# Gated linear attention and four experts in one kernel: hidden values moved by 128 bytes, K's right halves copied by GpSimd for six units, last stores in halves

## The chip, the cores and the metric

The kernel runs on one core of a Trainium2 chip. The metric is the time of one execution on the device in microseconds. Times of the kernel before are six runs: their median is 1057.78 us, the lowest 1056.80 and the highest 1058.26. A core has five engines with their own queues of instructions: TensorE (PE in the profile; PEld is its load of weights), VectorE (DVE), ScalarE (ACT), GpSimd (POOL) and SyncE (SP), which here does nothing but start transfers.

## What is computed

The first half is a gated linear attention: for each batch and head a state of 48 x 48 is scaled, row by row, with a gate, and a product of key and value is added; the output is the query times the state.

```python
# q, k, v, alpha: (4, 8, 768, 48), float32; alpha in 0.8 .. 1.0
for t in range(S):
    state = alpha[:, :, t, :, None] * state + einsum('bhd,bhe->bhde', k[:, :, t], v[:, :, t])
    y[:, :, t] = einsum('bhd,bhde->bhe', q[:, :, t], state)
```

The second half takes this output as 3072 rows `x` of 384 (8 heads of 48 side by side) and sends every row through four experts, whose results are added with normalised weights:

```python
# w1: (4, 384, 1024), w2: (4, 1024, 384)
p = domain_probs / (domain_probs.sum(-1, keepdims=True) + 1e-9)
for e in range(E):
    h = np.maximum(x @ w1[e], 0.0)
    out += p[:, e:e + 1] * (h @ w2[e])
```

## The kernel before

**Units and groups.** The sequence of 768 is cut into 6 chunks of 128 positions (`cb`); with 4 batches (`b`) this gives 24 *units* of 128 rows. `order` lists them chunk by chunk. The first group (`groups[0]`) holds 2 units, the next five hold 4 each, and the last (`LAST`, number 6) holds 2. A *task* is one expert on one group: `up` multiplies the group's `x` with `w1` and applies ReLU, `down` multiplies the hidden values with `w2`, and `add_up` adds the scaled result to the accumulator `acc`. The tasks of groups 0 to 4 follow one another; those of the last two groups alternate.

**Attention of a unit.** `attention(u)` is a generator. It transposes the gates, K and Q of all 8 heads on TensorE (`turned`, L270) into tiles `AT`, `KT` and `QT`, and then goes through seven levels of halving (`LEVELS`): on level `li`, blocks of `m` positions are joined in pairs. On each level `copy_q` (L321, ScalarE, two copies) copies the right halves of Q into a block tile `qb`, `next_q` (L328 and L330, VectorE) multiplies the right halves of Q and the gates with the gates of the left halves, and `next_k` (L341, VectorE) multiplies the left halves of K with the gates of the right halves. `next_k` writes a new `KT` tile, since TensorE still reads the old one, and so the right halves, which don't change, are copied over (L340). That is six copies of 128 x 256 elements for each unit. `products` (L348) multiplies K and Q of a level on TensorE, `take` (L358, VectorE) picks from the result by a mask, and `far` (L403) is the product of the highest level. `lat` holds the finished coefficients (L416, L421); `result` multiplies them with V and Q with the state (L443, `yps`), and L478 makes the product for the next state. The rows `x` go to `x_raw`.

**Order.** Engines work their queues in the order in which the program is written, and that order is written out by hand. For unit 0 and most of unit 1 it is a list of steps with idle products (`fill`) between them; TensorE has no other work then. From unit 1 on, the steps of an attention lie between the products of an expert task: `deal` gives each step a time from a table of costs, and `advance`, called with each product, inserts the steps that are due. So the attention of units 2 to 5, which are group 1, lies beside the experts of group 0, and so on. The weights are loaded once by SyncE (`load_piece`, L214 to L217), split by ScalarE and VectorE into three parts (`split_piece`, L226 to L232), and written by GpSimd's queue to device memory (L233, `kept<-w`); later groups load the split parts (L196, `w<-kept`). Raw pieces of `w2` lie in `hT` tiles of hidden values that aren't in use.

**In the experts.** L549 and L557 are the products with `w1` (`one`, `two`); L568, L570, L595 and L597 turn their sums into the hidden values `hT` in three parts (L551 for group 0, in one part), and L603 finishes the third. L650 is the product with `w2`, which takes 128 x 128 values of `hT` as the weights of TensorE and lets `w2` move through; L677 and L679 add up.

**Where tiles lie.** The pool `work` holds the tiles of the attention, `xT` and `x_raw`; the pool `hid` behind it holds `hT` and `acc`. In `work`, `x_raw` is the tile that is allocated last.

**Stores.** `add_up` puts the store of a finished unit on a list. The list is emptied in `up` of the next tasks, and what is left at the end of the program. GpSimd's queue starts the stores of groups 0 to 4, SyncE those of the last two.

Of the kernel before, what the change touches and what calls it, by code (L numbers as in the profile page):

```python
# [10 lines left out]
F32 = mybir.dt.float32  # L11
# [9 lines left out]
def kernel(  # L21
# [37 lines left out]
    nc = tc.nc  # L59

    B, H, S, D = q.shape
    E, DM, F = moe_w1.shape
    P = 128
# [5 lines left out]
    KC = DM // P  # L69
    FCH = F // P  # L70
    NT = B * P
# [6 lines left out]
    assert DM % P == 0 and F % (P * NQ) == 0 and DM <= 512 and KC * QF == FPQ * DM  # L78
    FINE = 1 + 1 / 4096
    TRIM = 1 - 1 / 8192  # L80

    j = np.arange(P)[:, None] % HALF
    n = np.arange(QUAD)[None, :]
# [7 lines left out]
    work = ctx.enter_context(tc.tile_pool(name="work", bufs=2))  # L91
# [20 lines left out]
    half = B // 2  # L112
    groups = [order[:half]] + [order[i:i + B] for i in range(half, len(order), B)]
    LAST = len(groups) - 1
# [20 lines left out]
    xraws = {}  # L135
# [4 lines left out]
    stores = deque()  # L140
# [80 lines left out]
    def split_piece(l, i):  # L221
# [3 lines left out]

        nc.scalar.activation(out=top, in_=whole, func=ACT.Copy, scale=TRIM)  # L226
        yield
        nc.scalar.activation(out=dif, in_=whole, func=ACT.Copy, scale=TRIM * 4096)
        yield
# [34 lines left out]
    def halves(t, m):  # L264
        return t.rearrange("p a (b two r) -> p a b two r", two=2, r=m)
# [7 lines left out]
    def attention(u):  # L273
# [15 lines left out]
        def own_terms():  # L289
            own = work.tile([P, NT], F32, name="t")[:, :H * D].rearrange("p (h d) -> p h d", d=D)  # L290
            nc.vector.tensor_mul(own, rq[:, :, :D], rk[:, :, :D])
            nc.vector.reduce_sum(out=dot, in_=own, axis=AX.X)
            load(after, "k")


        alone = u == 0
        if not alone:
            own_terms()
        yield
# [33 lines left out]
        def next_k(li):  # L333
            m = LEVELS[li]
            old = new = halves(KTs[li], m)
            if li + 1 < len(LEVELS):
                KTs.append(keys())
                new = halves(KTs[-1], m)
                copy = nc.gpsimd.tensor_copy if alone else nc.scalar.copy
                copy(out=new[:, :, :, 1, :], in_=old[:, :, :, 1, :])  # L340
            nc.vector.tensor_mul(new[:, :, :, 0, :], old[:, :, :, 0, :],  # L341
                                 spread(halved(decs[li])[:, :, :, 1], m))
# [24 lines left out]
        for li in range(3):  # L367
            copy_q(li)
            next_q(li)
            next_k(li)  # L370
            yield
# [6 lines left out]
        for li in range(4):  # L378
            products(li, banks[li // 2][:, li % 2])
        next_q(3)  # L380
        next_k(3)
        take(0, banks[0][:, 0])
        take(1, banks[0][:, 1])
        yield
        copy_q(4)
        next_q(4)
        next_k(4)
        take(2, banks[1][:, 0])
        take(3, banks[1][:, 1])
# [24 lines left out]
        for s in range(2):  # L414
            rows = slice(HALF * s, HALF * (s + 1))
            nc.scalar.copy(out=parts[:HALF, :, s, :, HALF:], in_=far[rows])  # L416
        yield
        for s in range(2):
            rows = slice(HALF * s, HALF * (s + 1))
            copy = nc.vector.tensor_copy if alone and s else nc.scalar.copy  # L420
# [8 lines left out]
        def result():  # L429
            yps = ps.tile([P, KC, P], F32, name="yps", tag="w")  # L430
            for c in range(KC):


                if c < 2:
                    now = [[(2 * c + j // 2, j % 2, (0, HD + TAIL)[j % 2], 2 * QUAD * (j % 2))
                            for j in range(4)]]
                    turns = ([(True, now[0])] if cb > 0 else []) + [(False, now[0])]
                else:
                    turns = [(True, [(p, 0, 0, QUAD) for p in range(NP)])] if cb > 0 else []
                    turns += [(False, [(p, i, QUAD + TAIL * i, 0) for p in range(NP)]) for i in range(2)]  # L440
                for n, (past, turn) in enumerate(turns):
                    for j, (p, i, in_v, in_st) in enumerate(turn):
                        nc.tensor.matmul(  # L443
                            yps[QUAD * j:QUAD * (j + 1), c, :],
                            lhsT=flat_st[:, p, in_st:in_st + QUAD] if past
                            else flat_v[:, p, in_v:in_v + QUAD],
                            rhs=QT[:, p, :] if past else lat[:, 2 * p + i, :],
                            start=(n == 0), stop=(n == len(turns) - 1))
            gi, slot = place[cb, b]
            if slot == 0:  # L450
                if gi == 0:
                    xTs[gi] = work.tile([P, 3, KC, NT], F32R, name="xT", bufs=1)
                    xraws[gi] = xTs[gi][:, 2].bitcast(F32)
                elif gi < LAST:
                    xraws[gi] = work.tile([P, KC, NT], F32, name="x_raw", bufs=1)
                else:
                    xraws[gi] = []
            if gi < LAST:
                nc.scalar.copy(out=xraws[gi][:, :, slot * P:(slot + 1) * P], in_=yps)
            else:  # L460

                xraws[gi].append(AT)
                nc.scalar.copy(out=AT[:, :KC, :], in_=yps)
# [6 lines left out]
        for step in (turn_keys, result) if u >= half else (result, turn_keys):  # L470
            step()
            yield

        if cb < NCB - 1:
# [5 lines left out]
            for i in range(2):  # L480
                rows = slice(HD * i, HD * (i + 1))
# [17 lines left out]
    def split_x(gi, step):  # L499
# [7 lines left out]
        for kc in range(KC) if step == 0 else [step - 1]:  # L507
# [3 lines left out]
            for x, out in pieces:  # L511
                if step == 0:
                    nc.scalar.activation(out=out[0], in_=x, func=ACT.Copy, scale=TRIM)
                else:
# [78 lines left out]
    def hidden_parts(x, parts):  # L593
        top, low, dif = parts
        nc.scalar.activation(out=top, in_=x, func=ACT.Relu, scale=TRIM)  # L595
        yield
# [13 lines left out]
    def down(gi, e, slots, between):  # L610
# [20 lines left out]
        for n, (side, slot, part, fc) in enumerate(steps):  # L631
            c, f = divmod(fc, FPQ)
            advance(cost(1, gi, e) * len(slots) / len(steps))
            while between and n >= between[0][0] * len(steps):
                between.popleft()[1]()
            if n and n % (len(steps) // (2 * len(slots))) == 0:
                background()
            if later and n % (len(steps) // 12 - 1) == len(steps) // 12 - 2:
                make_dif(*later.popleft())
            at = (side, slot)  # L640
            if n == begins[at]:
                sums[at] = ps.tile([P, DM], F32, name="ops", tag="g", bufs=4)
            h = hidden[c][:, :, f, slot * P:(slot + 1) * P]
            if part < 3:
                w = wt[1][first + c].rearrange("p t (c d) -> p t c d", d=DM)[:, part, f]
                h = h[:, part]
            else:
                w = wt[1][first + c].rearrange("p (c d) -> p c d", d=DM)[:, f]
                h = h[:, 2].bitcast(F32)
            nc.tensor.matmul(sums[at], lhsT=h, rhs=w, start=(n == begins[at]), stop=(n == ends[at]))  # L650
            if n == ends[at]:
                add_up(gi, e, slot, side, sums.pop(at))
# [14 lines left out]
    def add_up(gi, e, slot, kind, part):  # L667

        cb, b = groups[gi][slot]
        at = b * NCB + cb  # L670
        if e == 0 and (kind == 0 or not split2(gi, e)):
            accs[cb, b] = hid.tile([P, DM], F32, name="acc", bufs=B) if gi < LAST else \
                work.tile([P, NP * P], F32, name="QT")[:, :DM]
        acc = accs[cb, b]
        scale = (p_fine if kind == 0 else p_all)[:, at, e:e + 1]
        if e == 0 and (kind == 0 or not split2(gi, e)):
            nc.scalar.activation(out=acc, in_=part, func=ACT.Copy, scale=scale)  # L677
        else:
            nc.vector.scalar_tensor_tensor(out=acc, in0=part, scalar=scale, in1=acc,  # L679
                                           op0=ALU.mult, op1=ALU.add)  # L680
        if kind == 0:
            return
        if e == E - 1:
            del accs[cb, b]
            row = b * S + cb * P
            stores.append(lambda: (nc.sync if gi >= LAST - 1 else nc.gpsimd).dma_start(
                out=out[row:row + P, :], in_=acc))

# [43 lines left out]
    with tc.manual_schedule():  # L734
# [23 lines left out]
        def fill(n):  # L758
            for _ in range(n):
                nc.tensor.matmul(idle, lhsT=zeros, rhs=zeros, start=True, stop=True)  # L760

        runs = [attention(u) for u in range(len(groups[0]))]
        fill(7)
        for u, n in ((0, 2), (0, 3), (0, 4), (0, 5), (0, 5), (0, 4), (0, 3), (1, 0), (0, 0), (0, 2),
# [66 lines left out]
```

## Time and profile before

| | |
|---|---|
| Median of six runs | 1057.78 us (1056.80 to 1058.26) |
| The profiled execution | 1057.32 us, span 1055.5 us |
| Busy: TensorE, its weight loads | 1037.6 us, 903.2 us |
| Busy: VectorE, ScalarE, GpSimd | 781.8 us, 565.5 us, 35.5 us |
| Granted clock of TensorE | 1.000 |
| Transfers | 251.66 MB, mean 238 GB/s |

The profile is of one execution. The span reaches from its first to its last instruction; the execution is 1.82 us longer. In the lists, a line names its place in the kernel, the engine, the operation, what is written and read, and the shapes; behind the bar stand the busy time, the mean of one instruction in ns, and the idle time of the engine ahead of them with what ended it. In a timeline the first number is the start from the beginning of the span and the second the duration, both in us, and a bracket gives the idle time just before and what ended it. "SPq" is SyncE's queue.

How the busy time lies over the start (us in each stretch; the attention of units 0 and 1 fills the first two, that of units 2 to 5 lies in the next five):

| Stretch | PE | DVE | ACT | POOL | share of the transfer engines |
|---|---|---|---|---|---|
| 20 to 40 | 17.00 | 12.48 | 12.03 | 0.00 | 0.65 |
| 40 to 60 | 18.97 | 11.73 | 14.61 | 1.74 | 0.68 |
| 60 to 80 | 17.62 | 14.41 | 16.77 | 1.06 | 0.95 |
| 80 to 100 | 18.79 | 17.96 | 16.94 | 1.06 | 0.61 |
| 100 to 120 | 18.56 | 16.13 | 15.33 | 1.06 | 0.90 |
| 120 to 140 | 19.50 | 14.94 | 13.42 | 1.07 | 0.67 |
| 140 to 160 | 19.24 | 16.33 | 14.33 | 2.12 | 1.09 |

### The profile page before, as it was taken

To read this page: it belongs to the slowest core of one execution; us is meant where nothing else is said; L and a number is where in the kernel's file an instruction comes from. 1 tells how busy PE (TensorE), PEld (TensorE's weight loads), DVE (VectorE), ACT (ScalarE), POOL (GpSimd) and SP (SyncE) were. 2 spreads that over 40 slices of the span, in tenths; PEclk is the share of its full clock that TensorE was granted. 3 is DMA by queue.
4 is the path that set the end of the run, shared out by engine and by line. 5 is a ranking of instruction groups with operands and counts; after the bars stand their busy time and mean duration, and the time that the engine had idled before them with its cause. 6 is when DMAs were issued, how large, how long until landed. Compare 5 with 4: busy or idle time off the path is not lost.

```text
span 1055.5 us, 21578 instructions
## 1 busy us (share of the span) xinstructions
PE 1037.6 (98%) x8498; PEld 903.2 (86%) x8498; DVE 781.8 (74%) x1620; ACT 565.5 (54%) x1195; POOL 35.5 (3%) x77
## 2 busy tenths in 40 slices
PE   8899999999999999999999999999999999999998
PEld 8777777687877899898898898998989889898998
DVE  5578777668879778778877777986877875656565
ACT  4687876585665654445546536555474443323232
POOL 3000010000001000000000000000000000000000
PEclk9999999999999999999999999999999999999999
DMA  7696799997878956857759659586594454444531
GB/s 117 173 325 215 238 322 348 323 335 242 276 266 293 376 192 226 319 170 279 287 175 343 229 169 348 182 286 239 170 372 179 187 210 172 186 181 179 198 162 46
DMA packets 158838, 251.66 MB, mean 238 GB/s; under 512 B 120113, under 2 KB 135345, under 8 KB 136209
## 3 DMA queue, kind: packets, MB, share of 16 engines
q1 hardware_dynamic: 152688, 208.87, 58.0%
q0 software_dynamic: 5760, 41.29, 9.8%
q8 instruction: 67, 1.10, 0.4%
q14 instruction: 35, 0.28, 0.1%
q10 hardware_dynamic: 288, 0.12, 0.1%
HBM read 207.79 MB, written 42.47 MB: 237 GB/s over the span
## 4 chain that ended last, share of the span: by engine, by line
PE 85%; DVE 4%; ACT 4%; DMA 3%; SPq 2%; issue 1%; POOL 0%; ACTq 0%; DVEq 0%; POOLq 0%
PE ops L650 36%; PE one L557 23%; PE two L557 11%; PE sc L348 6%; PE yps L443 3%; PE tp L270 3%; DMA hT<-in_moe_w_dram 2%; ACT qb L321 1%; PE one L549 1%; PE sps L478 1%; PE far L403 1%; SPq L214 1%; DMA w<-in_moe_w_dram 1%; DVE w L230 1%; DVE near L358 1%
## 5 line engine op out<-in xcount | busy, mean ns | idle before, releaser
L650 PE MATMUL ops<-w,hT 128*128 128x384 f32 x1872 | 346.6, 340 | 0.2 <-DVE hT L603 0.2
L650 PEld LDWEIGHTS ops<-w,hT 128*128 128x128 f32 x1872 | 324.5, 188 | 4.7 <-ACT t L568 0.7
L557 PE MATMUL one<-xT,w 128*128 128x512 f32 x960 | 252.6, 398 | 0.9 <-DVE xT L252 0.5
L557 PEld LDWEIGHTS one<-xT,w 128*128 128x128 f32 x960 | 175.7, 188 | 39.2 <-ACT t L568 1.5
L568 ACT ACTIVATE t<-one 128x512 f32<-128x512 f32 (+1 forms) x192 | 107.0, 558 | 174.9 <-PE one L557 169.8
L321 ACT COPY qb<-QT 64x256 f32<-64x256 f32 x336 | 136.6, 406 | 73.7 <-DVE QT L300 40.9
L597 DVE SCALAR_TENSOR_TENSOR hT<-t,hT 128x512 fp32r<-128x512 f32 (+1 forms) x172 | 110.6, 643 | 68.2 <-ACT hT L595 65.7
L570 DVE TENSOR_TENSOR t<-t,two 128x512 f32<-128x512 f32 (+1 forms) x172 | 109.5, 637 | 57.7 <-ACT t L568 29.1
L595 ACT ACTIVATE hT<-t 128x512 fp32r<-128x512 f32 (+1 forms) x172 | 101.8, 592 | 85.7 <-DVE t L570 84.6
L557 PE MATMUL two<-xT,w 128*128 128x512 f32 x480 | 136.2, 392 | 0.0
L557 PEld LDWEIGHTS two<-xT,w 128*128 128x128 f32 x480 | 90.1, 188 | 20.0 <-DVE acc L679 0.3
L650 PE MATMUL ops<-hT 128*128 128x384 f32 x288 | 100.9, 491 | 0.3 <-DMA hT<-in_moe_w_dram 0.3
L603 DVE SCALAR_TENSOR_TENSOR hT<-hT 128x512 fp32r<-128x512 f32 (+1 forms) x172 | 101.0, 635 | 0.0
L358 DVE COPY_PREDICATED near<-masks,sc 128x256 f32<-128x256 uint8 x144 | 76.9, 534 | 19.2 <-PE sc L348 16.3
L328 DVE TENSOR_TENSOR QT<-QT,dec 128x256 f32<-128x256 f32 x144 | 61.2, 425 | 35.5 <-ACT qb L321 34.8
L348 PEld LDWEIGHTS sc<-qb,KT 128*64 128x64 f32 x2304 | 72.7, 138 | 9.3 <-issue 4.7
L348 PE MATMUL sc<-qb,KT 128*64 128x64 f32 x2304 | 77.2, 223 | 2.6 <-ACT qb L321 2.6
L650 PEld LDWEIGHTS ops<-hT 128*128 128x128 f32 x288 | 52.1, 190 | 29.6 <-DMA hT<-in_moe_w_dram 0.9
L679 DVE SCALAR_TENSOR_TENSOR acc<-ops,p_all,acc 128x384 f32<-128x384 f32 x82 | 49.9, 615 | 29.3 <-PE ops L650 28.2
L341 DVE TENSOR_TENSOR KT<-KT,dec 128x256 f32<-128x256 f32 x144 | 60.3, 419 | 0.0
L340 ACT COPY KT<-KT 128x256 f32<-128x256 f32 x138 | 57.5, 416 | 3.0
L549 PE MATMUL one<-xT,w 128*128 128x256 f32 (+1 forms) x240 | 46.9, 341 | 1.8 <-DMA w<-in_moe_w_dram 1.1
(90 smaller groups left out, 934.1 us busy)
## 6 DMA issues: line engine op xcount, KB each, us to landing
w<-kept SPq DMA_DIRECT2D x144, 1152.0 KB
kept<-w POOLq DMA_DIRECT2D x32, 1152.0 KB, 7.7
hT<-in_moe_w_dram SPq DMA_DIRECT2D x32, 384.0 KB
w<-in_moe_w_dram SPq DMA_DIRECT2D x48, 128.0 KB
ra<-in_alpha_dram SPq DMA_DIRECT2D x23, 192.0 KB
rk<-in_k_dram SPq DMA_DIRECT2D x23, 192.0 KB
rq<-in_q_dram SPq DMA_DIRECT2D x23, 192.0 KB
out_dram<-acc POOLq DMA_DIRECT2D x18, 192.0 KB, 7.0
```

Of the source, the lines that this page charges most:

```text
L321: nc.scalar.copy(out=qb[rows, :, i, :].rearrange("p a (b r) -> p a b r", r=m), in_=qv[rows])
L328: nc.vector.tensor_mul(qv, qv, spread(dv[:, :, :, 0], m))
L341: nc.vector.tensor_mul(new[:, :, :, 0, :], old[:, :, :, 0, :], spread(halved(decs[li])[:, :, :, 1], m))
L348: nc.tensor.matmul(out[HALF * s:HALF * (s + 1), 2 * p:2 * p + 2, :], lhsT=KTs[li][:, p, HALF * s:HALF * (s + 1)], rhs=qbs[li][:, p, :, QUA ...
L358: nc.vector.copy_predicated(near.rearrange("p a (b two r) -> p a b two r", two=2, r=m)[:, :, :, 1, :], mk.unsqueeze(1).broadcast_to([P, H, ...
L557: nc.tensor.matmul(out, lhsT=w[:, part, kc], rhs=x_part(gi, part, kc), start=(part == terms[0] and kc == 0), stop=(part == terms[-1] and k ...
L568: nc.scalar.activation(out=t, in_=one, func=ACT.Copy, scale=FINE)
L570: nc.vector.tensor_add(t, t, two)
L595: nc.scalar.activation(out=top, in_=x, func=ACT.Relu, scale=TRIM)
L597: nc.vector.scalar_tensor_tensor(out=low, in0=x, scalar=0.0, in1=top.bitcast(F32), op0=ALU.max, op1=ALU.subtract)
L603: nc.vector.scalar_tensor_tensor(out=dif, in0=top.bitcast(F32), scalar=1 / 4096.0, in1=low.bitcast(F32), op0=ALU.mult, op1=ALU.subtract)
L650: nc.tensor.matmul(sums[at], lhsT=h, rhs=w, start=(n == begins[at]), stop=(n == ends[at]))
```

## The change

Three edits. First, `x_raw` gets 32 more elements in each partition, of which nothing is used; the tiles of `hid`, that is `hT` (the values behind the ReLU) and `acc`, so lie 128 bytes further on. Second, `next_k` copies K's right halves with GpSimd for the units below `half + B` = 6, which are units 0 to 5, where it was unit 0 alone; the later units keep ScalarE. Third, the stores of the last group's two units are each cut into two of 64 rows, one on SyncE's and one on ScalarE's queue, and the stores of the group before it go to GpSimd's queue instead of SyncE's.

```diff
+    PAD = 32
...
         alone = u == 0
+        dense = u < half + B
...
-                copy = nc.gpsimd.tensor_copy if alone else nc.scalar.copy
+                copy = nc.gpsimd.tensor_copy if dense else nc.scalar.copy
                 copy(out=new[:, :, :, 1, :], in_=old[:, :, :, 1, :])
...
-                    xraws[gi] = work.tile([P, KC, NT], F32, name="x_raw", bufs=1)
+                    xraws[gi] = work.tile([P, KC * NT + PAD], F32, name="x_raw", bufs=1)[:, :KC * NT]
+                    xraws[gi] = xraws[gi].rearrange("p (c n) -> p c n", n=NT)
...
-            stores.append(lambda: (nc.sync if gi >= LAST - 1 else nc.gpsimd).dma_start(
-                out=out[row:row + P, :], in_=acc))
+
+            queues = (nc.sync, nc.scalar) if gi == LAST else (nc.gpsimd,)
+            for i, queue in enumerate(queues):
+                rows = slice(P // len(queues) * i, P // len(queues) * (i + 1))
+                stores.append(lambda queue=queue, rows=rows: queue.dma_start(
+                    out=out[row:row + P, :][rows], in_=acc[rows]))
```

## The prediction

> **What bounds the kernel now.** I read the first part of the page, then the chain that ended last in order of time, then the timeline of the stretches in which TensorE stood still.
>
> ```profile
> PE 1037.6 (98%) x8498; PEld 903.2 (86%) x8498; DVE 781.8 (74%) x1620; ACT 565.5 (54%) x1195; POOL 35.5 (3%) x77
> ...
> PE 85%; DVE 4%; ACT 4%; DMA 3%; SPq 2%; issue 1%; POOL 0%; ACTq 0%; DVEq 0%; POOLq 0%
> ...
> L340 ACT COPY KT<-KT 128x256 f32<-128x256 f32 x138 | 57.5, 416 | 3.0
> ```
>
> TensorE is busy for 98% of the span and carries 85% of the chain; ScalarE carries 4%. A change off TensorE can win at most what TensorE waits for. The third line is the group that the change takes from: 30 of its 138 copies belong to units 1 to 5. GpSimd is nearly empty.
>
> The places where TensorE waits (the bracket is the idle time before the instruction and what ended it):
>
> ```profile
> 61.33 0.69 PE L348 MATMUL sc<-qb,KT 128*64 128x64 f32 x16 [1.20 <-ACT qb L321]
> ...
> 77.87 1.08 PE L443 MATMUL yps<-lat,rv 128*32 128x128 f32 x32 [1.18 <-ACT lat L421]
> ...
> 81.74 0.69 PE L348 MATMUL sc<-qb,KT 128*64 128x64 f32 x16 [1.21 <-ACT qb L321]
> ...
> 118.99 0.43 PE L443 MATMUL yps<-lat,rv 128*32 128x128 f32 x8 [1.44 <-ACT lat L421]
> ...
> 140.54 0.43 PE L443 MATMUL yps<-QT,st 128*32 128x128 f32 x8 [0.48 <-DVE QT L300]
> ```
>
> Between 57 and 160 us, while group 0's experts run beside the attention of units 2 to 5, ScalarE ends four waits of together 5.03 us. Unit 1 (26 to 43 us) waits too, but there ScalarE's queue stands idle for VectorE: its copies of K's halves sit in slack. After 160 us the waits on TensorE are a few tenths each, and the change touches nothing there but the addresses and the stores.
>
> **GpSimd's copies.** Each copy takes 0.41 us on ScalarE; in its queue the next operation follows after 0.32 to 0.33 us, since neighbours overlap. So 30 copies free about 10 us of ScalarE, but only those inside a run of ScalarE without idle time ahead of a wait of TensorE shorten that wait:
>
> ```profile
> 76.24 0.44 ACT L340 COPY KT<-KT 128x256 f32<-128x256 f32 x1
> 76.57 1.24 ACT L421 COPY lat<-near 64x512 f32<-64x512 f32 x2
> 77.84 0.38 ACT L551 ACTIVATE hT<-one 128x256 f32<-128x256 f32 x1
> 78.24 0.84 ACT L228 ACTIVATE w<-w 128x768 fp32r<-128x768 f32 x1
> 78.99 0.80 ACT L321 COPY qb<-QT 64x256 f32<-64x256 f32 x2
> 79.81 0.41 ACT L340 COPY KT<-KT 128x256 f32<-128x256 f32 x1
> 80.13 0.38 ACT L551 ACTIVATE hT<-one 128x256 f32<-128x256 f32 x1
> ```
>
> - Wait at 61.33: one copy (59.42 to 59.73) stands between the last idle time and the Q copy that ends the wait; the copies before it are covered by VectorE's QT product, which the next Q copy needs anyway. Gain 0.31 us.
> - Wait at 77.87: the copy at 76.24 goes, `lat` starts 0.33 us earlier. Gain 0.33.
> - Wait at 81.74: the run has no idle time since 73.70, so the copy at 79.81 comes on top. Gain 0.32.
> - Wait at 118.99: copies at 114.11 and 116.95 lie in the run, 0.33 and 0.48 us to the next operation, 0.81 in all. I count it as given back, because the loads are next in line. From 105.31 to 139 us SyncE issues loads almost without a pause, single issues taking up to 3.4 us, and the read that VectorE needs for unit 5 is one of them:
>
> ```profile
> 121.78 3.37 SPq L215 DMA_DIRECT2D w<-in_moe_w_dram  x1
> ...
> 136.35 0.56 DVE L291 TENSOR_TENSOR t<-rq,rk 128x384 f32<-128x384 f32 x1 [2.48 <-DMA rq<-in_q_dram]
> ```
>
> VectorE waits 2.48 us for that load, goes through the queue behind it to L300, and L300 ends TensorE's wait at 140.54. What TensorE gains at 118.99 it waits longer at 140.54. The first three gains survive: the stream of loads starts at 105.31 on a release by TensorE (the state products, L478), so it moves with TensorE.
>
> Sum 0.31 + 0.33 + 0.32 = 0.96 us. At most: 0.96 + 0.81, and 0.98 for the waits at 140.54 (0.48) and 136.39 (0.50, ScalarE's ReLU) if the loads come earlier too, together 2.75.
>
> What is added: 30 copies of 0.41 us on GpSimd, 12.3 us, on an engine that is busy for 35.5 of 1055.5. They queue with the stores of split weights (L233, 16 of 0.53 us between 51 and 163 us), each of which waits for VectorE's split (L232). A copy behind one waits for an operation that VectorE has ahead of its own use of the copy (L341 of the next level), then 0.53 + 0.41 us, while VectorE does L328, L330 and L341 of the present level, three times 0.34: covered. If that cover goes, VectorE's next K product and TensorE's products behind it wait up to 0.9 us a time. The other cost is on VectorE. Unit 0 already runs this way, and its fourth copy met VectorE:
>
> ```profile
> 13.16 0.73 POOL L340 COPY KT<-KT 128x256 f32<-128x256 f32 x1 [0.90 <-DVE KT L341]
> ...
> 13.55 0.62 DVE L328 TENSOR_TENSOR QT<-QT,dec 128x256 f32<-128x256 f32 x1
> ```
>
> GpSimd took 0.73 instead of 0.41, VectorE 0.62 instead of 0.42. The L328 at 10.68 took 0.52 under a copy, the one at 12.13 took 0.43. That is 0.31 us of VectorE for six copies, 0.05 each; ends 0 and 0.20 a copy. I take 0 on the path at the mean, as VectorE idles after most of these steps (1.62 us before 116.96), and keep 24 x 0.20 = 4.8 us as the other end.
>
> The Trainium skill, in "SBUF — State Buffer", section "Who interferes with whom", says more: a VectorE instruction with two SBUF inputs and a GpSimd instruction that reads SBUF share a port pair under an exclusive lock, and the later one blocks until the other is done. By that rule every copy could hold VectorE for its whole 0.41 us, an estimate of 9.8 us for 24 copies, and the change would lose. The rows show the same kind of meeting at half that price at worst and an eighth on average, so the measurement is kept.
>
> **ReLU values 128 bytes further on.** `x_raw` grows by 32 elements, and what is allocated behind it, `hT` and `acc`, moves. No instruction is added. TensorE reads `hT` as weights in 1872 products of L650. Does their pace depend on where the bytes lie? Two full runs of 96 of them:
>
> ```profile
> 865.43 16.77 PE ops L650 x96
> ...
> 916.14 16.64 PE ops L650 x96
> ```
>
> 174.7 and 173.3 ns a product, and in every stage slots and parts of `hT` lie at other addresses. VectorE's steps on 512 elements take 684 to 694 ns whether they read `hT` (L603, L597) or only `t` and the sum (L570). So I take 0. Nothing here shows this very offset; the bound either way is the spread of those two runs, 1872 x 1.4 ns = 2.6 us.
>
> **Stores.** Unit stores of the last but one group go from SyncE to GpSimd: four issues at 1030.7 to 1034.8 us, 0.54 us each instead of 0.33, landing 7.0 us later, by 1042, while TensorE works until 1051.7. Nothing else is queued on GpSimd then and no load waits on SyncE: 0. Without that cover it would be 7 us. The very last store is on the path: VectorE ends at 1052.33, SyncE issues, waits 1.5 us for the landing, and then closes. In halves on two queues the same 192 KB go out, with two more semaphores to close. One issue takes 0.33 us either way. I take 0, with 0.3 us to either side (one issue saved or one more in front).
>
> The skill's "DMA: Bandwidth & Descriptors", section "Rules for kernel authors", advises against two transfers to disjoint partition halves, since they serialise; by it this part is worth nothing. No run here shows halves.
>
> **Sum.** The profiled execution took 1057.32 us, span 1055.5 and 1.82 around it. 1057.32 - 0.96 = 1056.36. The median of the runs lies 0.46 above the profiled execution, so 1056.8. About 0.2%, 2.1 us, is what a measurement of this kernel can tell from no change: 1055.7 to 1059.9 counts as the same.
>
> **Rivals.** (1) The relief carries through: the loads move with the released ScalarE (SyncE waited 4.8 us for these very copies), and all 2.75 us stay: 1057.78 - 2.75 = 1055.0. For it: three of the four waits are ScalarE's. Against: VectorE's 2.48 us for a load. (2) The new place of `hT` suits TensorE: 0.96 + 2.6 gives 1054.2. For it: the largest group of instructions reads it. Against: the even pace. (3) Slower: VectorE becomes the bound of units 2 to 5. In 80 to 100 us it is busy for 17.96 of 20, and each copy starts just when L328 of the same level is due. At 0.20 us for each of 24 copies, 4.8 - 0.96 gives 1061.6. It decides once a copy costs VectorE's path more than (2.1 + 0.96) / 24 = 0.13 us. For it: the pair at 13.55. Against: the mean of 0.05. (4) Part of the change does nothing: the halves, or the address. That is inside my forecast.
>
> **How the numbers follow.** Forecast 0.42, own range 1055.7 to 1058.4 (ScalarE's gain from nothing to all that is not given back, and the store's 0.3). Rival 1: 0.20; rival 2: 0.14; rival 3 and the bad side of the address, which alone would need 1.7 ns a product to be seen: 0.24. Faster 0.34, same 0.42, slower 0.24. The range reaches to 1053.6 (rival 2 and some of rival 1) and to 1061.2, short of rival 3 at its full price.
>
> **What would show it.** L340 with 36 copies on GpSimd and 108 on ScalarE, near 0.41 us each; the waits at 61, 78 and 82 us shorter by a third of a microsecond, that at 119 shorter and that at 140 longer; L650 at 173 to 175 ns; the close 3 us after VectorE's last step. I am wrong if L650's pace moves, if L328 and L341 grow by 0.1 us or more between 57 and 160 us, or if the waits at 78, 82 and 119 us disappear whole.

## The result and the profile after

The changed kernel takes 1055.48 us in the median of 18 runs (1054.66 to 1056.08), the kernel before in the runs beside it 1058.00 us (38 runs, 1056.53 to 1062.28). The ratio is 0.9974, 95% interval 0.9967 to 0.998: faster by a quarter of a per cent. The time lies inside the outer range (1053.6 to 1061.2 us), but 1.3 us below the forecast of 1056.8 and just below its own range (1055.7 to 1058.4). So what came is "faster", to which the prediction gave 0.34, and not "same", which it held likelier with 0.42. Its profiled execution took 1055.84 us, span 1054.0, against 1057.32 and 1055.5.

The line numbers moved: L650 is now L655, L557 is L562, L549 is L554, L340 is L344, L321 is L325, L328 is L332, L341 is L345, L443 is L447, L679 is L684; the stores are L695 and the loads of split weights L198.

From the page of the changed kernel: busy times, the chain that ended last, and two groups (products with `w2`, copies of K's right halves).

```profile
PE 1036.2 (98%) x8498; PEld 901.7 (86%) x8498; DVE 784.5 (74%) x1620; ACT 556.9 (53%) x1165; POOL 52.1 (5%) x111
...
PE 85%; DVE 5%; ACT 4%; SPq 2%; issue 2%; DMA 1%; POOL 0%; DVEq 0%; ACTq 0%; POOLq 0%
...
L655 PE MATMUL ops<-w,hT 128*128 128x384 f32 x1872 | 344.4, 340 | 0.2 <-DVE hT L608 0.2
...
L344 ACT COPY KT<-KT 128x256 f32<-128x256 f32 x108 | 45.0, 417 | 2.3
```

The copies went where they were to go: 30 fewer on ScalarE, which is busy for 8.6 us less, and GpSimd is busy for 16.6 us more. But the line that matters is the first group. The products with `w2` took 346.6 us before and take 344.4 now, with the same count and the same shapes; nothing in the program says that they should. The page of the kernel before has them, and the products with `w1`, so:

```profile
L650 PE MATMUL ops<-w,hT 128*128 128x384 f32 x1872 | 346.6, 340 | 0.2 <-DVE hT L603 0.2
...
L557 PE MATMUL one<-xT,w 128*128 128x512 f32 x960 | 252.6, 398 | 0.9 <-DVE xT L252 0.5
...
L557 PE MATMUL two<-xT,w 128*128 128x512 f32 x480 | 136.2, 392 | 0.0
```

How the waits of TensorE went, from the timeline of the changed kernel (places as in the prediction, and one more at the end):

```profile
61.18 0.69 PE L352 MATMUL sc<-qb,KT 128*64 128x64 f32 x16 [0.90 <-ACT qb L325]
77.55 1.08 PE L447 MATMUL yps<-lat,rv 128*32 128x128 f32 x32 [1.02 <-ACT lat L425]
81.33 0.69 PE L352 MATMUL sc<-qb,KT 128*64 128x64 f32 x16 [1.05 <-DVE w L232]
...
118.32 0.42 PE L447 MATMUL yps<-lat,rv 128*32 128x128 f32 x8 [1.08 <-ACT lat L425]
136.00 0.63 PE L272 MATMUL tp<-ident,rq 128*128 128x128 f32 x4 [0.60 <-DMA rq<-in_q_dram]
140.15 0.42 PE L447 MATMUL yps<-QT,st 128*32 128x128 f32 x8 [0.48 <-DVE QT L304]
163.78 1.62 PE L562 MATMUL one<-xT,w 128*128 128x512 f32 x6 [0.67 <-DVE dot L294]
```

The starts are what to compare: 61.33 became 61.18, 77.87 became 77.55, 81.74 became 81.33, 118.99 became 118.32, 140.54 became 140.15. So the changed kernel is ahead by 0.15, 0.32, 0.41, 0.67 and 0.39 us at these places. The last row is new. At 163.56 before, at 163.78 now, TensorE starts the first product that uses the split weights out of device memory (`w<-kept`). In the kernel before it follows without idle time:

```profile
160.72 3.07 PE L650 MATMUL ops<-hT 128*128 128x384 f32 x9
163.56 1.62 PE L557 MATMUL one<-xT,w 128*128 128x512 f32 x6
```

For the changed kernel the profile names a VectorE step, but of the things that this product waits for, the one that fits its start is the transfer, whose last part lands at 163.42 before and 163.65 now. The traces of all twelve kernels here that have this wait agree: the product starts 0.13 or 0.14 us after the last part has landed. From the issue of the load to that landing 9.9 to 11.8 us pass.

Since both programs run the same 8498 matmuls in the same order, the start of the k-th can be compared directly. This shows where time is won and lost (us, minus is earlier than in the kernel before; "copies alone" and "places and copies" are experiments further down, one trace each):

| at (us, before) | 57 | 62 | 83 | 120 | 153 | 164 | last product |
|---|---|---|---|---|---|---|---|
| after | 0.00 | -0.15 | -0.42 | -0.67 | -0.68 | +0.24 | -1.73 |
| copies alone | +0.11 | -0.03 | -0.30 | -0.59 | -0.53 | -0.16 | -0.16 |
| places and copies | -0.04 | -0.19 | -0.47 | -0.72 | -1.21 | -0.41 | -3.67 |

The changed kernel wins 0.68 us in the attention, loses 0.91 at the transfer, and then wins 1.97 us (0.24 + 1.73) bit by bit over the 890 us that follow. From the last step of VectorE to the end it takes 3.43 us instead of 3.22, which gives the 1.5 us between the spans. (Between the medians of the runs it is 2.5 us; the traces are one execution each.)

This slow gain is in L655's pace. From start to start, one product with `w2` follows the other after 174.52 ns before and 173.29 after (mean of the some 1730 neighbours that nothing lies between). 1872 x 1.23 ns = 2.3 us. The chain shows the same, in the runs of 96 such products towards the end. Before (the two that the prediction didn't show), then after:

```profile
966.80 16.77 PE ops L650 x96
1017.50 16.64 PE ops L650 x96
```

```profile
864.02 16.64 PE ops L655 x96
914.63 16.64 PE ops L655 x96
965.23 16.64 PE ops L655 x96
1015.83 16.64 PE ops L655 x96
```

Before, 16.77 and 16.64 take turns; after, every run is at 16.64.

### The profile page after: what moved, and what is told of

It reads as the page before. It is cut to its first block, busy times and chain, and to the rows that moved or that the text cites. A ratio compares the mean times of both kernels' runs of the same rounds, so it can differ in the third digit from the quotient of the medians.

```text
span 1054.0 us, 21611 instructions
## 1 busy us (share of the span) xinstructions
PE 1036.2 (98%) x8498; PEld 901.7 (86%) x8498; DVE 784.5 (74%) x1620; ACT 556.9 (53%) x1165; POOL 52.1 (5%) x111
## 4 chain that ended last, share of the span: by engine, by line
PE 85%; DVE 5%; ACT 4%; SPq 2%; issue 2%; DMA 1%; POOL 0%; DVEq 0%; ACTq 0%; POOLq 0%
PE ops L655 35%; PE one L562 23%; PE two L562 11%; PE sc L352 5%; PE yps L447 3%; PE tp L272 3%; PE one L554 2%; PE sps L483 1%; SPq L216 1%; ACT qb L325 1%; PE far L407 1%; DVE w L232 1%; DMA w<-in_moe_w_dram 1%; SPq L217 1%; DMA rq<-in_q_dram 1%
## 5 line engine op out<-in xcount | busy, mean ns | idle before, releaser
L655 PE MATMUL ops<-w,hT 128*128 128x384 f32 x1872 | 344.4, 340 | 0.2 <-DVE hT L608 0.2
L655 PEld LDWEIGHTS ops<-w,hT 128*128 128x128 f32 x1872 | 322.5, 188 | 4.8 <-ACT t L573 0.6
L562 PE MATMUL one<-xT,w 128*128 128x512 f32 x960 | 252.5, 398 | 1.6 <-DVE dot L294 0.7
L562 PEld LDWEIGHTS one<-xT,w 128*128 128x128 f32 x960 | 175.7, 188 | 40.1 <-ACT t L573 1.4
L325 ACT COPY qb<-QT 64x256 f32<-64x256 f32 x336 | 136.6, 407 | 81.0 <-DVE QT L304 41.1
L562 PE MATMUL two<-xT,w 128*128 128x512 f32 x480 | 136.3, 392 | 0.0
L562 PEld LDWEIGHTS two<-xT,w 128*128 128x128 f32 x480 | 90.0, 188 | 20.2 <-DVE acc L684 0.6
L655 PE MATMUL ops<-hT 128*128 128x384 f32 x288 | 100.9, 491 | 0.0
L332 DVE TENSOR_TENSOR QT<-QT,dec 128x256 f32<-128x256 f32 x144 | 62.0, 430 | 33.1 <-ACT qb L325 32.5
L655 PEld LDWEIGHTS ops<-hT 128*128 128x128 f32 x288 | 52.1, 190 | 29.4 <-DMA hT<-in_moe_w_dram 0.6
L684 DVE SCALAR_TENSOR_TENSOR acc<-ops,p_all,acc 128x384 f32<-128x384 f32 x82 | 49.9, 614 | 28.7 <-PE ops L655 27.7
L345 DVE TENSOR_TENSOR KT<-KT,dec 128x256 f32<-128x256 f32 x144 | 60.6, 421 | 0.0
L554 PE MATMUL one<-xT,w 128*128 128x256 f32 (+1 forms) x240 | 46.8, 341 | 1.7 <-DMA w<-in_moe_w_dram 1.0
L344 ACT COPY KT<-KT 128x256 f32<-128x256 f32 x108 | 45.0, 417 | 2.3
```

Of the source, the lines that this page charges most:

```text
L325: nc.scalar.copy(out=qb[rows, :, i, :].rearrange("p a (b r) -> p a b r", r=m), in_=qv[rows])
L332: nc.vector.tensor_mul(qv, qv, spread(dv[:, :, :, 0], m))
L554: nc.tensor.matmul(one, lhsT=w[:, kc], rhs=xraws[gi][:, kc, lo:hi], start=(kc == 0), stop=(kc == KC - 1))
L562: nc.tensor.matmul(out, lhsT=w[:, part, kc], rhs=x_part(gi, part, kc), start=(part == terms[0] and kc == 0), stop=(part == terms[-1] and k ...
```

## The experiments

Each is the kernel before with the edit shown; the runs of the kernel before that it is compared with were made beside it.

**The change in its three parts.** First the moved `hT` alone:

```diff
+                    xraws[gi] = work.tile([P, KC * NT + PAD], F32, name="x_raw", bufs=1)[:, :KC * NT]
```

> The kernel before with the 128 bytes alone: x_raw wider by 32 elements, hT and acc 128 bytes further on. Theory A (the place of hT sets the pace of the products with w2): L650's pace falls from 174.5 to 173.3 ns a product as in the changed kernel, 1872 x 1.1 ns = 2.0 us; ratio to before 0.9981, and with no other part of the change it is the largest gain of the three. Theory B (ScalarE's relief is the gain, and the pace of that one profile is chance): pace 174 to 175 ns, ratio 1.000.

Measured: ratio 0.9978 [0.9965, 0.9992], 1055.46 us against 1057.66; L650's pace 173.30 ns. 1058 x 0.0022 = 2.3 us; within the intervals this is the whole gain of the change. Its profiled execution is the slowest of its 11 runs (1058.92 us), and shows one way in which executions differ:

```profile
165.71 2.81 PE L559 MATMUL one<-xT,w 128*128 128x512 f32 x6 [2.52 <-DMA w<-kept]
```

Here this product starts 2.2 us later than before, and TensorE stands still for 2.52 us; here the profile names the transfer itself. After this pause the granted clock of TensorE is 0.50 from 166 to 168 us and 0.69 from 168 to 170, and the six products take 2.81 us where the kernel before had 1.62: at 175 us the kernel is 3.7 us behind.

Then GpSimd's copies alone:

```diff
+        dense = u < half + B
-                copy = nc.gpsimd.tensor_copy if alone else nc.scalar.copy
+                copy = nc.gpsimd.tensor_copy if dense else nc.scalar.copy
```

> The kernel before with GpSimd's copies of K's right halves for units 0 to 5 alone. Theory A: TensorE is 0.6 to 0.9 us early at 153 us and waits again at 163.5 us for the first split piece of w1 from device memory, so nothing is left: ratio 0.9995 to 1.0005, L650 at 174 to 175 ns. Theory B: the early 0.7 to 1 us stays, or grows to the 2.6 us that the runs show: ratio 0.9975 to 0.999.

Measured: 1.0006 [0.9995, 1.0016]; the pace stays at 174.53 ns. The trace is the second row of the table: 0.53 us ahead at 153 us, 0.16 after the transfer. That is what theory A expected, down to the pace.

And the stores alone:

```diff
+            queues = (nc.sync, nc.scalar) if gi == LAST else (nc.gpsimd,)
```

> The kernel before with the stores alone: last group's in halves on two queues, those of the group before it on GpSimd's. Theory A: the time from VectorE's last step to the end of the span grows from 3.22 to 3.4 us as in the changed kernel; ratio 1.0002. Rival: in runs without the profiler the two queues land earlier, 0.3 us or more, ratio 0.9997 or less.

Measured: 1.0007 [0.9998, 1.0016]. The time from VectorE's last step to the end is 3.42 us, as after the change, and 3.21 to 3.23 in the kernels with whole stores. The last two stores, in the timelines of the kernel before and of this one (SyncE's queue; the second row of this one is ScalarE's):

```profile
1050.96 1.73 SPq L686 DMA_DIRECT2D out_dram<-QT  x2
1051.71 0.62 DVE L679 SCALAR_TENSOR_TENSOR QT<-ops,p_all,QT 128x384 f32<-128x384 f32 x1 [0.78 <-PE ops L650]
```

```profile
1051.59 1.90 SPq L689 DMA_DIRECT2D out_dram<-QT  x2
1051.60 1.89 ACTq L689 DMA_DIRECT2D out_dram<-QT  x2
1052.34 0.62 DVE L679 SCALAR_TENSOR_TENSOR QT<-ops,p_all,QT 128x384 f32<-128x384 f32 x1 [0.77 <-PE ops L650]
```

The last issue ends 0.36 us after VectorE with a whole store (1052.69 and 1052.33), and 0.53 with halves (1053.49 and 1052.96): one issue of the whole takes 0.33 us, the two of halves, which run at the same time, 0.50 and 0.51. Whether the smaller number of rows or the second queue makes them longer wasn't separated. The last part lands 1.88 us after VectorE's last step with a whole store, 2.45 with halves, which land one behind the other (by 1055.15 and by 1055.41). The close behind the last landing is shorter with halves, 0.97 us against 1.34; together that is the 0.2 us.

**Which property of the address counts?** In the allocation of the kernel before, every piece of `w1` and `w2` begins 416 bytes above a multiple of 512, and `xT` and `hT` both 480 bytes above one; after the change `hT` begins at 96. All steps inside these tiles (slots, parts, columns) are multiples of 512 bytes, so all products of a line share one place. Two theories: the place against a fixed boundary, or the distance between the two operands of a product. Two runs tell them apart. In the first, `xT` moves with `hT` (the padding goes into a tile ahead of `xT`):

```diff
-            dec = work.tile([P, NP, P // (2 * m)], F32, name=f"dec{li}", bufs=1)
+            n = NP * P // (2 * m)
+            dec = work.tile([P, n + XPAD * (li == 6)], F32, name=f"dec{li}", bufs=1)[:, :n]
+            dec = dec.rearrange("p (a r) -> p a r", a=NP)
```

with `XPAD = 32`, 128 bytes.

> The kernel before with the 128 bytes put ahead of xT, so that xT, x_raw, hT and acc all move. In the products with w1 (L557) xT moves through TensorE against w1 as weights, and their pace before lies between 226 and 232 ns, mean 229.7. Theory A1 (the place of the one operand against the other, or against a boundary of 512 bytes, costs a few ns): L557 falls towards 226 ns as L650 does towards 173, 1440 x 3 ns = 4 us more than the shift of hT alone; ratio 0.994 to 0.995. Theory A2 (only the place of hT, which TensorE loads as weights, matters): L557 unchanged, ratio as with hT alone, 0.998.

In the second, a padding of 128 bytes in a constant tile (`qb3`) ahead of everything moves the weights' pieces and the attention's tiles along, so that all places change and no distance does.

> The kernel before with 128 bytes put ahead of the weights too: w, AT, KT, xT, x_raw and hT all move by 128, so every tile keeps its distance to the others. Theory R (the distance between the start of the operand loaded as weights and the start of the one moving through, taken modulo 512 bytes, sets the pace): L650 174.5 ns, L557 229 to 230 ns, ratio 1.000. Theory M (the place of one operand by itself): hT and xT lie as in the run with xT moved, so L650 at 173.3 and L557 at 233, ratio 1.002.

Measured: 1.0022 [1.0013, 1.003] and 1.0019 [1.0008, 1.0031]. In the first, neither A1 nor A2 had the time: both expected a gain. From the page of the first of the two, the products with `w2` and the two groups with `w1`:

```profile
L653 PE MATMUL ops<-w,hT 128*128 128x384 f32 x1872 | 344.6, 340 | 0.1
L560 PE MATMUL one<-xT,w 128*128 128x512 f32 x960 | 255.6, 401 | 1.2 <-DVE dot L293 0.5
L560 PE MATMUL two<-xT,w 128*128 128x512 f32 x480 | 138.1, 396 | 0.0
```

Against before, -2.0 us, +3.0 (from 252.6) and +1.9 (from 136.2): +2.9, and the span is 2.7 longer. The products with `w1` react to `xT` as those with `w2` do to `hT`. In the second kernel the paces are those of before, 174.93 ns with `w2` and 229.99 and 229.06 with `w1` (before 229.62 and 228.68). So the distance decides, not the place. The ratio by itself would have spoken for the place, for which 1.002 had been expected; but in its trace this kernel is slower for another reason, the wait for the first split piece again:

```profile
166.30 1.63 PE L559 MATMUL one<-xT,w 128*128 128x512 f32 x6 [2.38 <-DMA w<-kept]
```

TensorE is 2.7 us behind there, of 4.3 at the last product; the granted clock stays at 1.00 here. That the other runs of this kernel lose their time at the same place is not shown.

**Which distances, and with what period?** The edit that moves `xT` and `hT`, with `XPAD` 112 (both tiles at the place of `w`, distance 0), 8 (both on a multiple of 512) and 64 (both 256 bytes on).

> The kernel before with 448 bytes ahead of xT: xT and hT now start at 416 modulo 512, as the weights w do, distance 0. The products of KT with w1 already lie so, at 119.3 ns for 256 columns, 12.6 ns over 256 columns at full clock. Theory R: L557 at 226 ns and L650 at 172.6 ns (the same 12.6 over 213.3 and 160), 1440 x 3.3 + 1872 x 1.9 = 8.3 us, ratio 0.992. Theory M: no such gain in both at once; either moves by itself.

> The kernel before with 32 bytes ahead of xT: xT and hT start on a boundary of 512 bytes. Theory M, as a rule of alignment (an operand that starts on a boundary is read without a loss): L557 at 226 and L650 at 173 ns or less, 1440 x 3.3 + 1872 x 1.5 = 7.6 us, ratio 0.993. Theory R: distance 96 modulo 512 for both, between the 64 of the kernel before and the 192 that the changed kernel has in L650; L650 near 174, L557 229 or more, ratio 0.999 to 1.002.

> The kernel before with 256 bytes ahead of xT: xT and hT start at 224 modulo 512. Theory R: weights minus moving is 192 in L557, as it is in L650 of the changed kernel, so L557 falls to 226 to 227 ns; in L650 it is 320, as it was in L557 with xT moved by 128, so L650 rises to 177 to 178 ns; together 1440 x -3 + 1872 x 3.5 = +2.2 us, ratio 1.002. Theory M with boundaries of 256 bytes: 224 is 480 less 256, nothing changes, ratio 1.000.

Measured: 0.9965 [0.9953, 0.9978], 1.0044 [1.0032, 1.0057] and 1.0000 [0.9986, 1.0014]. The first gains, as the theory of the distance had it, but less than half of what I expected (0.992); the second is slower than either theory had it. The last was a miss for the distance modulo 512: 256 bytes change nothing (174.66, 229.83 and 228.84 ns, against 174.52, 229.62 and 228.68), so the period is 256 bytes and not 512. The place against a boundary of 256 bytes would also have given 1.000, but it doesn't fit the paces of the run in which everything moves. That both tiles on a multiple of 512 give the slowest kernel of all (174.64, 233.23 and 232.62 ns) also speaks against the theory of the place as a rule of alignment.

**The best places.** With the period of 256: `XPAD = 48` puts `xT` at distance 0 from `w`, 48 more elements in `x_raw` put `hT` at distance 192. No other part of the change.

> The kernel before with two paddings and nothing else of the change: xT moves up by 192 bytes and hT by 384, so that xT starts 0 bytes and hT 192 bytes from the pieces of w, both counted modulo 256 (modulo 512 xT is 256 bytes away, a place not run so far). Theory of the distance modulo 256: L557 at 228.9 and 228.3 ns from start to start as in the run with xT and hT at 416, L650 at 173.3 ns as after the change; against before 1872 x 1.2 ns = 2.3 us and 960 x 0.7 ns + 480 x 0.4 ns = 0.9 us, so 1054.0 to 1054.8 us, ratio 0.9965 to 0.997 (a shade below the run at 416, by 1872 x 0.5 ns = 0.9 us). If the period were 512 bytes: L557 could be anything from 228 to 233 ns; at 233 ns the 1440 products cost 5 us and the ratio is about 1.001.

Measured: 1054.51 us (1053.76 to 1054.63), ratio 0.9954 [0.994, 0.9967]; paces 173.33, 229.12 and 228.19 ns. Time and paces are as expected; the ratio is lower than expected, since the kernel before took 1058.35 us beside it. The groups of its page:

```profile
L655 PE MATMUL ops<-w,hT 128*128 128x384 f32 x1872 | 344.5, 340 | 0.2 <-DVE hT L608 0.2
...
L562 PE MATMUL one<-xT,w 128*128 128x512 f32 x960 | 251.7, 397 | 1.5 <-DVE xT L254 0.6
...
L562 PE MATMUL two<-xT,w 128*128 128x512 f32 x480 | 135.5, 390 | 0.0
```

-2.1, -0.9 and -0.7 us. The place 256 bytes from `w`, not run before, gives the pace of distance 0, which confirms the period. All kernels by distance (start of the tile that is loaded as weights minus start of the tile that moves, modulo 256; mean from start to start in ns):

| distance | products with `w2`, 384 columns | products with `w1`, 512 columns (`one` / `two`) |
|---|---|---|
| 0 | 173.77 | 228.89 / 228.27, 229.06 / 228.09, 229.12 / 228.19 |
| 64 | 174.51 to 175.11 in seven kernels | 233.16 / 233.33 |
| 96 | 174.64 | not run |
| 160 | not run | 233.23 / 232.62 |
| 192 | 173.29 to 173.38 in five kernels | 229.52 / 228.46 to 230.19 / 229.29 in nine kernels |

At 192 the pace of the products with `w2` is even from stretch to stretch of the trace (about 173 to 173.5 ns), at 64 it wanders between 173.3 and 176.7. The kernel in which everything moves shows it, in its runs of 96:

```profile
868.68 16.96 PE ops L652 x96
919.58 16.64 PE ops L652 x96
970.63 16.96 PE ops L652 x96
1021.59 16.77 PE ops L652 x96
```

So the distance decides whether the pace can be slow; what picks the pace of one stretch at a slow distance is open. The products with `w1` aren't even at their 192 either: in the kernel without the wait, the next one below, they go from 228.4 ns to 233.4 between 900 and 980 us, at a granted clock of 1.00.

**Does the transfer at 163.5 us swallow the copies' gain?** A kernel without that wait: the split `w1` of the last expert is not written to device memory, and the later groups read the last but one expert's in its place, so that the loads of group 1 need not wait for the write (and the output is another).

```diff
-        nc.gpsimd.dma_start(out=kept[l][i % (E * NQ)], in_=w.bitcast(F32))
+        if l == 1 or i < (E - 1) * NQ:
+            nc.gpsimd.dma_start(out=kept[l][i % (E * NQ)], in_=w.bitcast(F32))
...
+            k -= NQ * (l == 0 and e == E - 1)
             nc.sync.dma_start(out=w.bitcast(F32), in_=kept[l][k])
```

> The kernel before; the split first-layer weights of the last expert are not written to device memory in the first group, and the later groups read the last but one expert's in their place (so the output is another). This takes some 1.15 MB x 4 of stores out of the stretch before 163 us, and the loads of group 1's first pieces need not wait for them. Theory that the wait at 163.5 us is for these loads: the first of L557's products of 512 columns starts 0.5 to 1 us earlier than before's 163.6 us, the second to fourth piece no longer wait (before, 18.5 us lie between the first and the last product of the four pieces), and the end comes 1 to 2 us earlier: ratio 0.998 to 0.999. Rival, that VectorE's work (the dot products that the profile names there) sets that start: nothing moves, 1.000.

> The run before this one and GpSimd's copies for the units beside the first group; nothing else of the change. Theory that the copies gain 0.5 to 0.7 us until 153 us and the load wait at 163.5 us absorbs it: here, without that wait, TensorE stays 0.5 to 0.7 us ahead of the run without the copies through 164 us and to its last product; the ratio is 0.0005 lower than that run's, which only the traces can tell. Rival, that the copies' gain is lost to VectorE or ScalarE in the attention beside the next group whatever the loads do: ahead by 0.5 at 153 us and by 0 to 0.2 at the end.

Measured: 0.998 [0.997, 0.999] without the copies and 0.9982 [0.9973, 0.999] with them; medians 1056.97 and 1056.95 us, of 12 runs each. The wait is gone: the first load is issued at 149.47 us instead of 153.48, and the product starts at 161.61 instead of 163.56. The ratio is as expected, but the gain did not come where I expected it. Without the copies TensorE is 1.72 us ahead already at 153 us, of which 0.31 lie before 57 us and 1.40 come between 128 and 153 us, and nothing is added at 164. The kernel with the copies is ahead of it by 0.22 us at 57 us, by 0.91 at 120, and by 0.06 at 141, as if both had come to the same bound. From there to 821 us they differ by 0.04 to 0.13 us. So my theory, that without the transfer at 163.5 us the gain would last, fell. The rival, that it is lost in the attention whatever the loads do, had the end right (0 to 0.2 us), but not the way: it expected 0.5 us at 153 us, and there only 0.06 is left. Nor is VectorE or ScalarE shown to be the reason: the kernel with copies stands 0.3 us at 136 us for Q's rows (`rq`), the other doesn't. (Of the last products nothing can be said: the kernel without copies lost 1.9 us between 821 and 1000 us, where its pace with `w2` went to 176.7 ns at distance 64 and that with `w1` to 233.4.)

Last, the best places and the copies together, the stores whole:

> The two paddings (xT 0 and hT 192 bytes from the pieces of w, modulo 256) with GpSimd's copies, stores whole. Theory that the load wait absorbs the copies: as with the paddings alone, 1054.0 to 1054.8 us, the last product within 0.2 us of that run's. Rival, that the copies' 0.5 us carries through: 0.5 us earlier at the last product.

Measured: 1054.15 us (1053.72 to 1054.54), ratio 0.9952 [0.9937, 0.9967], against 0.9954 without the copies. It is the fastest kernel here, but from the places alone it can't be told. In its trace the last product is 0.93 us ahead of that other kernel's, of which 0.31 lie before the copies begin; the first load of a split piece was issued 1.17 us earlier (152.29 and 153.46 us), and the product that waits for it started 0.96 us earlier (163.14 and 164.10). In this pair the kernel with the copies stays ahead, but one pair doesn't show that the copies did it: in kernels without copies the same load was issued at 152.64 to 154.36 us.

## Why the prediction was right or wrong

**GpSimd's copies.** The mechanism of the early waits was right and the sum was wrong. Two steps failed. The first is the addition of the early waits, 0.31 + 0.33 + 0.32 by 82 us, with VectorE's part put at 0 on the path: measured 0.41. The product at 61.33 came 0.29 us earlier against the one ahead of it, near the 0.31 of its term, but that one, at 59.45, had come 0.14 later. The rows of the changed kernel ahead of it:

```profile
58.12 0.50 DVE L332 TENSOR_TENSOR QT<-QT,dec 128x256 f32<-128x256 f32 x1 [0.27 <-ACT qb L325]
...
58.55 0.50 DVE L334 TENSOR_TENSOR dec<-dec 128x128 f32<-128x128 f32 x1
58.66 0.83 ACT L325 COPY qb<-QT 64x256 f32<-64x256 f32 x2 [0.57 <-DVE QT L332]
```

Before, these two steps took 0.43 and 0.29 us, and the Q copy began at 58.58. The wait at 77.87 came 0.32 us earlier, as its own term says, but the 0.15 won at 61 was no longer in it. The rows show where it went, in the changed kernel:

```profile
73.55 0.38 ACT L556 ACTIVATE hT<-one 128x256 f32<-128x256 f32 x1 [1.32 <-PE one L554]
...
73.95 0.84 ACT L228 ACTIVATE w<-w 128x768 fp32r<-128x768 f32 x1
...
74.16 0.74 DVE L332 TENSOR_TENSOR QT<-QT,AT 128x256 f32<-128x256 f32 x1
74.17 0.43 POOL L344 COPY KT<-KT 128x256 f32<-128x256 f32 x1
```

ScalarE's split step starts at 73.95 (before 73.98) although its ReLU ahead of it is 0.15 us earlier, and the run from which `lat` follows begins there anew. And VectorE's L332 took 0.74 us beside a copy, 0.32 more than its 0.42 alone. The second failed step is that the early gains survive because the loads "move with TensorE". Up to 120 us the gain is the copies' own: from 57 to 120 us the four kernels with copies come 0.67 to 0.70 us earlier against the kernel before, and the nine others without them move by no more than 0.03. From there on the traces no longer tell them apart: between 120 and 153 us the kernels without copies win 0.03 to 1.73 us against the kernel before, those with them -0.06 to 0.56. And at 163.5 us the lead no longer counts, since the product there waits for the last part of the first load of a split piece: 163.65 us in the changed kernel, 0.23 later than before. The prediction named waits "of a few tenths" after 160 us and looked no further; this one became the wait that mattered once TensorE came early. That at 118.99 us would be given back at 140.54 held in part: 0.67 of gain at 120 us, 0.39 at 141, and a row for `rq` with 0.60 us at 136. Over the runs the copies are worth nothing that was measured: 1.0006, 1056.95 against 1056.97, 1054.15 against 1054.51, and 1055.48 with the whole change against 1055.46 with the moved `hT` alone. Whether some tenths remain stays open.

**VectorE as the bound (rival 3).** VectorE did become slower. Between 57 and 160 us, its groups before and after:

```profile
L328 DVE TENSOR_TENSOR QT<-QT,dec 128x256 f32<-128x256 f32 x27 | 11.5, 425 | 11.2 <-ACT qb L321 10.8
L341 DVE TENSOR_TENSOR KT<-KT,dec 128x256 f32<-128x256 f32 x27 | 11.3, 419 | 0.0
L330 DVE TENSOR_TENSOR dec<-dec 128x128 f32<-128x128 f32 (+5 forms) x27 | 5.4, 200 | 0.0
L374 DVE TENSOR_TENSOR near<-ident,dot 128x512 f32<-128x512 f32 x5 | 3.4, 686 | 0.0
```

```profile
L332 DVE TENSOR_TENSOR QT<-QT,dec 128x256 f32<-128x256 f32 x27 | 12.1, 447 | 8.8 <-ACT qb L325 8.6
L345 DVE TENSOR_TENSOR KT<-KT,dec 128x256 f32<-128x256 f32 x27 | 11.7, 433 | 0.0
...
L334 DVE TENSOR_TENSOR dec<-dec 128x128 f32<-128x128 f32 (+5 forms) x27 | 6.3, 235 | 0.0
...
L378 DVE TENSOR_TENSOR near<-ident,dot 128x512 f32<-128x512 f32 x5 | 3.8, 761 | 0.0
```

Together 31.6 us became 33.9: 2.3 us for some 24 copies, 0.1 each, between the 0.05 that the prediction took at the mean and the 0.20 of its other end, and below the 0.13 from which the rival would decide. (The worst single step, the 0.32 at 74.16, lies above that end.) It stays within VectorE's idle time (11.2 us before L328, 8.8 after), as was said. The lock of the Trainium skill's "SBUF — State Buffer", section "Who interferes with whom", by which the prediction had estimated 9.8 us, would be four times what these rows show.

**The moved `hT`.** This step failed, and it is the one that mattered: "I take 0". Rival 2, with a chance of 0.14, was the mechanism, at 2.3 of the 2.6 us of its bound. The prediction looked at the right rows and read them wrongly. It took 16.77 and 16.64 us for a spread about one pace, and argued that slots and parts of `hT` lie at other addresses in every stage. They do, but all of them at steps of 512 bytes, which for this effect is no difference. What it didn't look at was the allocation: how far the two operands lie apart. It had named the sign of its error, "I am wrong if L650's pace moves". The bound from the two rows held.

**The stores.** "One issue takes 0.33 us either way" is wrong: the halves take 0.50 and 0.51. The 0.2 us of loss lies within the 0.3 that was kept. The move of the group before the last to GpSimd cost nothing, its rows are hidden as said. From the Trainium skill's rule on halves ("DMA: Bandwidth & Descriptors", section "Rules for kernel authors"), that they serialise, the prediction took nothing for this part; the halves did land one behind the other, and the run shows a small cost.

**The sum.** In the trace: 0.68 by 153 us, less 0.91 at the transfer, 1.97 behind it, near the 2.3 of the pace, less 0.21 at the end: 1.5 us. The prediction's 0.96 came from the copies alone. The range held because it reached to rival 2. The reason for being in it was not the forecast's: as far as the forecast goes, that was luck.

## What to carry to other kernels

Where TensorE carries the chain, compute its pace from start to start for each line of products, and compare it between neighbours and between kernels: 0.7% of pace over 1872 products was worth more than all that came of the waits that this change set out to shorten. Before arguing that an address can't matter, write down where both operands of a product start and the steps inside them; a padding of some hundred bytes a partition is all that it takes to try. And a wait that is shortened early is only won if nothing that follows has a time of its own: look for the next transfer that TensorE meets within a few tenths, not only for the next wait that is long. Before you call a few tenths in a trace a gain, see how far traces of kernels without the change lie apart at the same place.

## What the hardware showed that I had not expected

The pace of fp32r products (128 x 128 weights) depends on the distance between the weights' and the moving operand's starts in SBUF, modulo 256 bytes: mean over a trace 173.3 to 175.1 ns at 384 columns, 228.1 to 233.3 ns at 512. Distances 0 and 192 are fast and 64 is slow for both, 96 is slow for the first and 160 for the second. What in the chip makes it so was not tried, and distances other than these five were not run.

Two stores of 64 rows, issued on two queues at the same time, took longer to issue than one of 128 rows: 0.53 us from VectorE's end to the issue's end, against 0.36.
